# Attention with a top-128 MLP: the exponentials split at column 1024, the TensorE transposes moved up among the scores, weighted sums five blocks behind the scores, query tiles of 512 columns

## The chip, the cores and the metric

The kernel runs on one core of a Trainium2 chip. The metric is the device time of one execution in microseconds; of several executions the median counts. TensorE does matmuls (PE in the profile, its weight loads are PEld), VectorE is DVE, ScalarE is ACT, GpSimd is POOL, and SyncE (SP) issues the DMAs.

## The reference

Four images are attended to, each with N = 12288 queries of C = 128 and 768 keys. The keys, which are the values too, are the 4x4 means of `kv`, projected. Then, for each image, the 128 rows with the highest gate score go through an MLP.

```python
kv_pool = kv.reshape(B, H // r, r, W // r, r, C).mean(axis=(2, 4))
k = v = kv_pool.reshape(B, -1, C) @ w_sr
s = scale * (q @ k.transpose(0, 2, 1))
a = np.exp(s - s.max(-1, keepdims=True))
a /= a.sum(-1, keepdims=True) + 1e-09
x = a @ v                                        # (4, 12288, 128)
scores = np.einsum('bsd,d->bs', x, w_gate)
out = x.copy()
for b in range(B):
    top_idx = np.argpartition(-scores[b], capacity)[:capacity]   # capacity = 128
    xe = x[b, top_idx]
    ye = np.maximum(xe @ w1, 0.0) @ w2
    g = 1.0 / (1.0 + np.exp(-scores[b, top_idx]))
    out[b, top_idx] = xe + g[:, None] * ye
```

## The kernel before

A block is 256 queries (`QT` = 2 groups of 128). An image has 48 blocks, the program 192, which one loop takes in order. Each turn of the loop holds steps of three different blocks.

**The scores of block i+1** (`S`, tile `s`) go into one of two PSUM buffers of three banks, 1536 columns wide: columns 0 to 767 are the first 128 queries against 768 keys, 768 to 1535 the second. Four parts are written one after the other: part 3 (1024:1536), 2 (768:1024), 1 (512:768), 0 (0:512). Each part is three matmuls, since the queries and the keys are split into a high f32r and a low bf16 half (`qh`, `ql`, `kh`, `kl`; `kb` is the key in bf16): `kl,qh`, `kb,ql` and `kh,qh`; parts 2 and 0 do `kh,qh` first.

**The weights of block i.** `s_max` (DVE, tile `m`) takes the maximum of each row over all 1536 columns. Three exponentials on ACT follow: part 1 is 768:1280 into `am`, part 2 is the last 256 columns (1280:1536), part 0 is 0:768 into `am`. `CUT` is 1280. In the first three images (`by_pe`, 144 blocks) part 2 goes into a tile `ae`, and TensorE transposes it in two steps (`turn_pe`, `s<-cst,ae`) back into the PSUM columns 1280:1536. ACT casts these to f16 and DVE takes the bf16 rest (`at<-s`, `at<-s,at`): these weights then stand in the tile `at` already transposed. The other 1280 columns are cast to f16 on ACT (`hl<-am`), POOL subtracts for the bf16 rest (`hl<-am,hl`), and two DMA transposes (`turn`) bring both halves into `at`. In the last image the DMA transposes all 1536 columns, and TensorE transposes none.

**The weighted sums of block i-4** (`AV`, tile `o_two`): 36 matmuls with the transposed weights from `at` as stationary and the values `vx` as moving operand. `LAG` is 4, and `at` has 5 buffers. DVE then normalises (`rz`, `x`), and every second block a DMA stores 512 rows.

**Queries.** `qraw` are tiles of 2048 columns (8 blocks) in two buffers. Every second block one DMA of 512 columns is to load its quarter of a tile, eight blocks ahead.

**Around it.** Steps of four other jobs are put in at named points of the loop (`at_point`): the next image's keys (`next_keys`: loads, 4x4 sums on POOL, projection on TensorE) and values (`v_split`), and for the image before, the search for the top 128 (`topk`: an integer key per row, two searches by bits, each a compare and count on DVE and a matmul, then `pick`) and the MLP. The PSUM room of these jobs is in the score buffer that is not in use (`borrow`).

The order on PE, DVE, ACT and POOL is the order of the program: `InOrder` chains each instruction to the one before it on its engine, and since it is the helper through which all of them go, they all stand at L52 in the profile. DMAs don't go through it: a scheduler sets the order of SP's queue from the buffers' dependencies.

After the loop a tail takes the sums of the last blocks into borrowed PSUM areas (`dest`, `spare`), and then the last image's search and MLP, with nothing beside them.

Of the kernel before, what the change touches and what calls it, by code (L numbers as in the profile page):

```python
# [6 lines left out]
F32 = mybir.dt.float32  # L7
# [9 lines left out]
HALF = 256  # L17
PSUM = bass.MemoryType.PSUM

P = 128  # L20
B, N, C = 4, 12288, 128
HK, WK, R = 384, 32, 4
M = (HK // R) * (WK // R)
KT = M // P
TAPS = R * R
CHUNK = 2048
JPC = CHUNK // P
NCH = N // CHUNK
QT = 2
BLK = QT * P  # L30
NBLK = N // BLK
BPC = CHUNK // BLK
VC = C + 2
# [33 lines left out]
def attention_topk_mlp(ctx, tc, a, outs, capacity):  # L67
    nc = tc.nc
# [4 lines left out]
    kvp = ctx.enter_context(tc.tile_pool(name="kvp", bufs=3))  # L73
    kvs = ctx.enter_context(tc.tile_pool(name="kvs", bufs=2))
    keys = ctx.enter_context(tc.tile_pool(name="keys", bufs=2))
    qp = ctx.enter_context(tc.tile_pool(name="qp", bufs=2))
    qs = ctx.enter_context(tc.tile_pool(name="qs", bufs=3))
    wk = ctx.enter_context(tc.tile_pool(name="wk", bufs=3))
    wke = ctx.enter_context(tc.tile_pool(name="wke", bufs=2))
    hlp = ctx.enter_context(tc.tile_pool(name="hlp", bufs=4))  # L80
    at = ctx.enter_context(tc.tile_pool(name="at", bufs=5))
    ob = ctx.enter_context(tc.tile_pool(name="ob", bufs=3))
    sm = ctx.enter_context(tc.tile_pool(name="sm", bufs=4))
    tk = ctx.enter_context(tc.tile_pool(name="tk", bufs=2))
# [44 lines left out]

    qraw = {}  # L130

    def load_q(b, ch, lo=0, hi=CHUNK):
        if (b, ch) not in qraw:
            qraw[b, ch] = qp.tile([P, CHUNK], F32, name="q_raw")
        nc.sync.dma_start(out=qraw[b, ch][:, lo:hi], in_=a["q"][:, b, ch, lo:hi])

    kvset = {}

# [75 lines left out]

    def first_keys():
        new_keys(0)
        load_q(0, 0, 0, 2 * BLK)
        raws = [load_kv(0, kc) for kc in range(3)]
        nc.sync.dma_start(out=cst, in_=a["cst"])
        raws += [load_kv(0, kc, 2) for kc in range(3, KT)]  # L220
        load_q(0, 0, 2 * BLK, CHUNK)
        split_q(0, 0)
        kv = kvset[0]
        for kc in range(KT):
# [93 lines left out]
    xt_ = {}  # L318

    def split_q(b, blk):  # L320
        ch, h = divmod(blk, BPC)
        raw = qraw[b, ch][:, h * BLK:(h + 2) * BLK]
        qh = qs.tile([P, 2 * BLK], F32R, name="qh")
        ql = qs.tile([P, 2 * BLK], BF16, name="ql")
        act.copy(qh, raw)
        pool.tensor_tensor(out=ql, in0=raw, in1=qh.bitcast(F32), op=ALU.subtract)
        for i in range(2):
            h, l = (x[:, i * BLK:(i + 1) * BLK] for x in (qh, ql))
            qsplit[b, blk + i] = h, h.bitcast(BF16).rearrange("p (q s) -> p q s", s=2)[:, :, 1], l
# [23 lines left out]
    def by_pe(n):  # L353
        return blocks[n][0] < B - 1

    def exp(n, part):
        lo, hi, j = ((0, M, 0), (M, CUT, 1), (CUT, 2 * M, 1))[part]
        if part == 1:
            st[n]["a"] = wk.tile([P, CUT], F32, name="am")
            st[n]["hl"] = hlp.tile([P, 2, QT * M], U16, name="hl")  # L360
            st[n]["at"] = at.tile([P, 2, QT * KT, P], U16, name="at")
        s = s_flat[n % 2][:, lo:hi]
        if part == 2:
            out = s
            if by_pe(n):
                out = st[n]["ae"] = wke.tile([P, HALF], F32, name="ae")
        else:
            out = st[n]["a"][:, lo:hi]
        r = act.activation(out, s, AF.Exp, bias=st[n]["m"][:, j:j + 1])
        if part == 0:  # L370
            st[n]["exp0"] = r.ins
            if "low" in st[n]:
                tc.declare_no_dep(r.ins, st[n]["low"], reason="both only read, other banks")

    def turn_pe(n):
        for c in range(2):
            lo = CUT + c * P
            r = pe.transpose(s_flat[n % 2][:, lo:lo + P], st[n]["ae"][:, c * P:(c + 1) * P], ident)
            tc.declare_no_dep(r.ins, st[n]["exp0"], reason="other banks")

    def halves(n, part):
        lo, hi = ((0, CUT), (CUT, 2 * M))[part]
        a = s_flat[n % 2][:, lo:hi] if part else st[n]["a"]
        if part and by_pe(n):
            hl = [st[n]["at"][:, h, CUT // P:].rearrange("p t q -> p (t q)") for h in range(2)]
        else:
            hl = [st[n]["hl"][:, h, lo:hi] for h in range(2)]
        return a, hl[0].bitcast(F16), hl[1].bitcast(BF16)
# [238 lines left out]

    start(vals, first_values())
    nb = len(blocks)
    LAG = 4  # L630
    for i in range(nb):
        old = i >= LAG
        b, blk = blocks[i]
        if blk % 2 == 0 and i + BPC < nb:
            nb_, nblk = blocks[i + BPC]
            load_q(nb_, nblk // BPC, nblk % BPC * BLK, (nblk % BPC + 2) * BLK)
        if blk == 0 and b + 1 < B:
            start(prep, next_keys(b + 1))
        if i:
# [20 lines left out]
        bank0 = list(InOrder.seen)  # L660
        if more:
            S(i + 1, (3,), bank0 + bank1)
            S(i + 1, (2,), bank0)
        exp(i, 1)
        exp(i, 2)
        if by_pe(i):
            exp(i, 0)
            turn_pe(i)
        if more:
            S(i + 1, (1,), bank0)  # L670
            S(i + 1, (0,))
        to_high(i, 1)
        if old:
# [1 line left out]
            recip(i - LAG)  # L675
            finish(i - LAG)
        to_low(i, 1, dve)
        if not by_pe(i):
            exp(i, 0)
        to_high(i, 0)  # L680
        turn(i, 0)
        to_low(i, 0, pool)
# [8 lines left out]
    n = nb - 1  # L691
    b = blocks[n][0]
    spare = [s_buf[(n + 1) % 2][:, 2 * k:2 * k + 2].rearrange("p k q -> p (k q)")[:, 0:QT * VC].rearrange("p (j c) -> p j c", j=QT) for k in range(3)]
    dest = {n - 3: o_all, n - 2: spare[0], n - 1: spare[1], n: spare[2]}

    def out(m):
        for j in range(QT):
# [20 lines left out]
    for j in range(3):  # L718
        pool.memset(jt[:, j:j + 1], float(j + 1))

    for m in (n - 3, n - 2):
        out(m)
        norm(m)
        put(m)
# [84 lines left out]
```

## Time and profile before

| | us |
|---|---|
| median of three runs (977.23 to 986.22) | 981.31 |
| profiled execution, its own time | 983.61 |
| its span in the trace | 981.8 |
| PE busy | 908.2 |
| PEld busy (beside PE) | 729.7 |
| POOL busy | 749.9 |
| ACT busy | 729.5 |
| DVE busy | 699.7 |

The engines' rows are busy times, so what an engine waits for is not in them. The reduction `m` on DVE runs once a block, and the distance from one `m` to the next is called a block's period here.

### The profile page before, as it was taken

The numbers are of one execution on the slowest core, as the hardware profiler recorded it, in microseconds if no ns is written. First come the engines' busy times: TensorE is split into PE (matmuls) and PEld (weight loads), VectorE is DVE, ScalarE is ACT, GpSimd is POOL, SyncE is SP. The second block draws the span as 40 slices with busy tenths as digits, with TensorE's granted clock in tenths as the row PEclk, the third lists the DMA queues.
The fourth block names the chain that finished last, engine by engine and source line by source line (L and its number), as shares of the span: only waits on it lengthen the run. The fifth ranks groups of instructions, "written<-read, shape, count | busy, mean of one in ns | idle before, by whom it ended". The sixth has DMA issues, their size and how long they took to land.

```text
span 981.8 us, 26115 instructions
## 1 busy us (share of the span) xinstructions
PE 908.2 (93%) x10067; PEld 729.7 (74%) x10067; DVE 699.7 (71%) x1732; ACT 729.5 (74%) x1177; POOL 749.9 (76%) x573
## 2 busy tenths in 40 slices
PE   3889999999989999998999998999999999999944
PEld 2668777787768787776787876877787887777743
DVE  6456666666668777776767776777768887878674
ACT  2567887877967877877877866878789988988700
POOL 1478889888778988987888887898778877777600
PEclk9999999999989999999999999999999999999966
DMA  9999999999999999999989999999999999999910
GB/s 357 227 190 220 241 220 224 244 242 236 225 203 186 249 226 219 233 230 225 235 169 210 236 218 226 207 199 203 199 184 245 224 242 244 231 235 234 225 40 6
DMA packets 600508, 211.31 MB, mean 215 GB/s; under 512 B 532288, under 2 KB 582592, under 8 KB 599616
## 3 DMA queue, kind: packets, MB, share of 16 engines
q1 hardware_dynamic: 600128, 209.12, 104.4%
q8 instruction: 79, 1.29, 0.6%
q0 software_dynamic: 256, 0.52, 0.2%
q14 instruction: 45, 0.37, 0.1%
HBM read 52.04 MB, written 25.43 MB: 79 GB/s over the span
## 4 chain that ended last, share of the span: by engine, by line
PE 56%; DVE 13%; ACT 9%; DMA 8%; issue 4%; POOL 3%; SPq 1%; POOLq 0%; ACTq 0%; DVEq 0%
PE s L52 31%; PE o_two L52 25%; DVE m L52 8%; DMA at<-hl 7%; ACT am L52 5%; POOL hl L52 1%; DVE junk L52 1%; ACT ae L52 1%; ACT hl L52 1%; ACT at L52 1%; POOL ql L52 1%; DVE at L52 1%; DMA xe<-out,idx 1%; POOL kv_sum L52 1%; ACT s L52 1%
## 5 line engine op out<-in xcount | busy, mean ns | idle before, releaser
L52 POOL TENSOR_TENSOR hl<-am,hl 128x1280 bf16<-128x1280 f32 x192 | 503.7, 2623 | 153.6 <-ACT hl L52 75.4
L52 PEld LDWEIGHTS <-at 128*128 128x128 f16 (+1 forms) x6912 | 415.5, 97 | 71.4 <-DMA at<-hl 22.5
L52 PE MATMUL o_two<-vx,at 128*128 128x130 f16 x6804 | 435.0, 220 | 17.5 <-DMA at<-hl 12.9
L52 ACT ACTIVATE am<-s,m 128x512 f32<-128x512 f32 (+1 forms) x384 | 305.4, 795 | 140.6 <-DVE m L52 80.9
L52 DVE TENSOR_REDUCE m<-s 128x2 f32<-128x1536 f32 x192 | 337.1, 1756 | 24.8 <-PE s L52 20.8
L52 PE MATMUL s<-kl,qh 128*128 128x512 bf16 (+1 forms) x768 | 253.3, 333 | 0.0
L52 PE MATMUL s<-kh,qh 128*128 128x512 f32 (+1 forms) x768 | 251.8, 409 | 0.0
L52 PE MATMUL s<-kb,ql 128*128 128x512 bf16 (+1 forms) x768 | 248.7, 327 | 0.5 <-POOL ql L52 0.4
L52 ACT CAST hl<-am 128x1280 f16<-128x1280 f32 x192 | 245.1, 1276 | 1.5
L52 DVE TENSOR_TENSOR at<-s,at 128x256 bf16<-128x256 f32 x144 | 61.1, 425 | 132.5 <-ACT at L52 124.4
L52 PEld LDWEIGHTS s<-kh,qh 128*128 128x128 f32 x768 | 131.6, 192 | 30.5 <-issue 0.6
L52 POOL TENSOR_TENSOR ql<-q_raw,qh 128x512 bf16<-128x512 f32 x96 | 122.5, 1276 | 6.8 <-ACT qh L52 6.8
L52 PEld LDWEIGHTS <-qh 128*128 128x128 bf16 x768 | 75.3, 98 | 63.2 <-issue 62.4
L52 DVE TENSOR_TENSOR x<-o_two,rz 128x260 f32<-128x260 f32 x189 | 81.0, 429 | 10.0
L52 PEld LDWEIGHTS <-ql 128*128 128x128 bf16 x768 | 76.2, 99 | 3.7 <-POOL ql L52 1.1
L52 DVE TENSOR_SCALAR rz<-o_two,sg 128x2 f32<-128x2 f32 x189 | 41.1, 218 | 40.2 <-PE o_two L52 39.3
L52 PE MATMUL s<-cst,ae 128*128 128x128 f32 x288 | 61.6, 296 | 8.4 <-ACT ae L52 7.7
L52 ACT ACTIVATE ae<-s,m 128x256 f32<-128x256 f32 x144 | 67.3, 467 | 0.0
L52 ACT CAST at<-s 128x256 f16<-128x256 f32 x144 | 54.5, 379 | 16.4 <-PE s L52 15.0
L52 ACT CAST qh<-q_raw 128x512 fp32r<-128x512 f32 x96 | 60.6, 631 | 1.1 <-DMA q_raw<-in_q 1.1
L52 PEld LDWEIGHTS s<-cst,ae 128*128 128x128 f32 x288 | 30.4, 141 | 32.0 <-ACT ae L52 31.4
L52 POOL TENSOR_TENSOR kv_sum<-kv_raw 128x256 f32<-128x256 f32 x72 | 52.4, 727 | 0.0
(164 smaller groups left out, 557.4 us busy)
## 6 DMA issues: line engine op xcount, KB each, us to landing
out<-x SPq DMA_DIRECT2D x96, 256.0 KB, 3.4
q_raw<-in_q SPq DMA_DIRECT2D x93, 256.0 KB, 3.8
kv_raw<-in_kv SPq DMA_DIRECT2D x36, 512.0 KB, 5.4
kv_raw<-in_kv SPq DMA_DIRECT2D x6, 1024.0 KB, 7.4
at<-hl SPq DMA_TRANSPOSE x384, 4.0
w<-in_w SPq DMA_DIRECT2D x2, 512.0 KB
q_raw<-in_q SPq DMA_DIRECT2D x1, 768.0 KB, 7.6
cst<-in_cst SPq DMA_DIRECT2D x1, 320.0 KB
```

Of the source, the lines that this page charges most:

```text
L52: r = f(*args, **kwargs)
```

## The change

Three things are changed.

1. In the first three images the exponentials are split into 1024:1536 (512 columns), 768:1024 (256) and 0:768, all into `am`, which is now 1536 columns wide; `ae` and its pool are gone. The two TensorE transposes come right behind score part 3 of the next block and read `am`; score parts 2, 1 and 0 follow them. Exponential 0:768 moves on ACT behind the cast `at<-s`, and behind DVE's subtraction in the program. In the last image the splits stay as they were.
2. `LAG` is 5 instead of 4, `at` has 6 buffers, and the tail does one more block.
3. Each 512 query columns are a tile of their own (four buffers of 512 instead of two of 2048).

```diff
-    qp = ctx.enter_context(tc.tile_pool(name="qp", bufs=2))
+    qp = ctx.enter_context(tc.tile_pool(name="qp", bufs=4))
-    wke = ctx.enter_context(tc.tile_pool(name="wke", bufs=2))
-    at = ctx.enter_context(tc.tile_pool(name="at", bufs=5))
+    at = ctx.enter_context(tc.tile_pool(name="at", bufs=6))
...
-    def load_q(b, ch, lo=0, hi=CHUNK):
-        if (b, ch) not in qraw:
-            qraw[b, ch] = qp.tile([P, CHUNK], F32, name="q_raw")
-        nc.sync.dma_start(out=qraw[b, ch][:, lo:hi], in_=a["q"][:, b, ch, lo:hi])
+    def load_q(b, blk):
+        ch, h = divmod(blk, BPC)
+        qraw[b, blk] = qp.tile([P, 2 * BLK], F32, name="q_raw")
+        nc.sync.dma_start(out=qraw[b, blk], in_=a["q"][:, b, ch, h * BLK:(h + 2) * BLK])
...
     def exp(n, part):
-        lo, hi, j = ((0, M, 0), (M, CUT, 1), (CUT, 2 * M, 1))[part]
+        early = by_pe(n)
+        lo, hi, j = ((0, M, 0), (M, 1024 if early else CUT, 1), (1024 if early else CUT, 2 * M, 1))[part]
...
+        out = s if part == 2 and not early else st[n]["a"][:, lo:hi]
         r = act.activation(out, s, AF.Exp, bias=st[n]["m"][:, j:j + 1])
...
     def turn_pe(n):
+        st[n]["apart"] = []
         for c in range(2):
             lo = CUT + c * P
-            r = pe.transpose(s_flat[n % 2][:, lo:lo + P], st[n]["ae"][:, c * P:(c + 1) * P], ident)
-            tc.declare_no_dep(r.ins, st[n]["exp0"], reason="other banks")
+            r = pe.transpose(s_flat[n % 2][:, lo:lo + P], st[n]["a"][:, lo:lo + P], ident)
+            st[n]["apart"].append(r.ins)
...
-    LAG = 4
+    LAG = 5
...
             S(i + 1, (3,), bank0 + bank1)
-            S(i + 1, (2,), bank0)
-        exp(i, 1)
-        exp(i, 2)
+        exp(i, 2 if by_pe(i) else 1)
         if by_pe(i):
-            exp(i, 0)
             turn_pe(i)
+        exp(i, 1 if by_pe(i) else 2)
         if more:
-            S(i + 1, (1,), bank0)
+            S(i + 1, (2, 1), bank0)
             S(i + 1, (0,))
         to_high(i, 1)
...
         to_low(i, 1, dve)
-        if not by_pe(i):
-            exp(i, 0)
+        exp(i, 0)
         to_high(i, 0)
...
-    dest = {n - 3: o_all, n - 2: spare[0], n - 1: spare[1], n: spare[2]}
+    spare.append(s_buf[n % 2][:, 4:6].rearrange("p k q -> p (k q)")[:, 0:QT * VC].rearrange("p (j c) -> p j c", j=QT))
+    dest = {n - 4: o_all, n - 3: spare[0], n - 2: spare[1], n - 1: spare[2], n: spare[3]}
...
-    for m in (n - 3, n - 2):
+    for m in range(n - LAG + 1, n - 1):
```

What stands on TensorE in one ordinary block, before. `s_110` is the score buffer that the next block's scores go into and `s_111` the one of the block in hand; `cst` holds the identity for a transpose. The waits in brackets name the engine.

```order
L52 MATMUL s_110<-kh,qh 128x512
L52 MATMUL s_110<-kh,qh 128x256
L52 LDWEIGHTS qh
L52 MATMUL s_110<-kl,qh 128x256
L52 LDWEIGHTS ql
L52 MATMUL s_110<-kb,ql 128x256
L52 MATMUL s_111<-cst,ae 128x128 [waits DVE_49,Activation_49]
L52 MATMUL s_111<-cst,ae 128x128
L52 LDWEIGHTS qh
L52 MATMUL s_110<-kl,qh 128x256
```

And the same place after, where the buffers are called `s_107` and `s_108`.

```order
L52 MATMUL s_107<-kh,qh 128x512
L52 MATMUL s_108<-cst,am 128x128 [waits Activation_49]
L52 MATMUL s_108<-cst,am 128x128
L52 MATMUL s_107<-kh,qh 128x256
L52 LDWEIGHTS qh
L52 MATMUL s_107<-kl,qh 128x256
L52 LDWEIGHTS ql
L52 MATMUL s_107<-kb,ql 128x256
L52 LDWEIGHTS qh
L52 MATMUL s_107<-kl,qh 128x256
```

The two transposes stood behind the three matmuls of score part 2; now they stand ahead of them, right behind part 3, and read the tile of the first exponential instead of the second one's.

What stands on ACT in one block, before.

```order
L52 ACTIVATE am<-s_110,m 128x512 [waits DVE_49,Pool_49]
L52 ACTIVATE ae<-s_110,m 128x256
L52 ACTIVATE am<-s_110,m 128x768
L52 CAST at<-s_110 128x256 [waits PE_49]
L52 CAST hl<-am 128x1280 [waits DMAHW5_49,DMAHW4_49,Activation_49]
```

And after.

```order
L52 ACTIVATE am<-s_107,m 128x512 [waits DVE_49,Pool_49]
L52 ACTIVATE am<-s_107,m 128x256
L52 CAST at<-s_107 128x256 [waits PE_49]
L52 ACTIVATE am<-s_107,m 128x768
L52 CAST hl<-am 128x1280 [waits DMAHW7_49,DMAHW6_49,Activation_49]
```

The cast `at<-s` stood behind the 768-column exponential; now it stands ahead of it, and the large exponential comes just ahead of the large cast.

What stands in SP's queue where the queries are loaded, before.

```order
L402 DMA_TRANSPOSE at<-hl 128x10x128 x2
L135 DMA q_raw<-in_q 128x512 x4
L402 DMA_TRANSPOSE at<-hl 128x10x128 x2
L438 DMA out<-x 128x4x128
L402 DMA_TRANSPOSE at<-hl 128x10x128 x4
L438 DMA out<-x 128x4x128
```

And after.

```order
L134 DMA q_raw<-in_q 128x512
L434 DMA out<-x 128x4x128
L398 DMA_TRANSPOSE at<-hl 128x10x128 x4
L134 DMA q_raw<-in_q 128x512
L434 DMA out<-x 128x4x128
L398 DMA_TRANSPOSE at<-hl 128x10x128 x4
```

The four query loads of a 2048-column tile stood in one bunch between two blocks' transposes, since its buffer comes free at once; now one load stands in every two blocks.

## Rows read from the trace of the kernel before

**Rows 1.** The page's own parts 1 and 2: the span, the busy time of each engine, and the busy share of the DMA engines in 40 equal slices of the span (9 is 90% or more).

```profile
span 981.8 us, 26115 instructions
PE 908.2 (93%) x10067; PEld 729.7 (74%) x10067; DVE 699.7 (71%) x1732; ACT 729.5 (74%) x1177; POOL 749.9 (76%) x573
DMA  9999999999999999999989999999999999999910
```

**Rows 2.** The table by windows, all instructions. The columns: the window in us, its length, then the busy time (and count) of PE, PEld, DVE, ACT and POOL, the granted TensorE clock as a share of full speed, the DMA share and GB/s. The second window begins at the `m` of block 5 and ends at that of block 144, the third ends at that of block 191; the last is the tail.

```profile
60.35:715.73 655.38, 639.33 (x7151) 510.75 (x7149) 471.92 (x1062) 512.60 (x837) 558.48 (x432) 0.99 1.10 220
715.73:921.54 205.81, 200.18 (x2332) 162.53 (x2330) 162.35 (x384) 182.43 (x274) 158.81 (x101) 1.00 1.16 228
```

**Rows 3.** The timeline of one ordinary block, cut to DVE's `m`, ACT, and the matmuls and weight loads around the TensorE transposes. The columns: start in us, how long, engine, line, operation, out<-in, shapes, count; in brackets the idle time just before and what ended it.

```profile
91.92 1.76 DVE L52 TENSOR_REDUCE m<-s 128x2 f32<-128x1536 f32 x1
...
93.78 0.69 ACT L52 ACTIVATE am<-s,m 128x512 f32<-128x512 f32 x1 [0.68 <-DVE m L52]
...
94.36 0.47 ACT L52 ACTIVATE ae<-s,m 128x256 f32<-128x256 f32 x1
...
94.57 0.28 PE L52 MATMUL s<-kl,qh 128*128 128x256 bf16 x1
...
94.69 0.27 PE L52 MATMUL s<-kb,ql 128*128 128x256 bf16 x1
94.72 0.90 ACT L52 ACTIVATE am<-s,m 128x768 f32<-128x768 f32 x1
94.88 0.20 PEld L52 LDWEIGHTS s<-cst,ae 128*128 128x128 f32 x2 [0.20 <-ACT ae L52]
...
95.16 0.27 PE L52 MATMUL s<-kl,qh 128*128 128x256 bf16 x1
...
95.50 0.38 ACT L52 CAST at<-s 128x256 f16<-128x256 f32 x1
...
95.75 1.29 ACT L52 CAST hl<-am 128x1280 f16<-128x1280 f32 x1
95.92 0.42 DVE L52 TENSOR_TENSOR at<-s,at 128x256 bf16<-128x256 f32 x1 [0.99 <-ACT at L52]
...
96.37 1.76 DVE L52 TENSOR_REDUCE m<-s 128x2 f32<-128x1536 f32 x1
```

**Rows 4.** Groups of weight loads of the whole span, by shape: count, then busy us and mean ns of one, then idle time before them and what ended it.

```profile
L52 PEld LDWEIGHTS s<-kh,qh 128*128 128x128 f32 x768 | 131.6, 192 | 30.5 <-issue 0.6
L52 PEld LDWEIGHTS s<-cst,ae 128*128 128x128 f32 x288 | 30.4, 141 | 32.0 <-ACT ae L52 31.4
```

**Rows 5.** The table of waits of the whole span: the waiting engine, tile and line, then what it waited for, the sum in us, how often, the longest.

```profile
PEld s L52 <- ACT ae L52: 31.4, 112, 3.8
...
PEld L52 <- DMA at<-hl: 22.5, 29, 2.7
...
PE o_two L52 <- DMA at<-hl: 12.9, 22, 2.2
```

**Rows 6.** The timeline around block 120: a bunch of query loads on SP, and two waits of TensorE's weight loads in that block.

```profile
593.17 2.22 SPq L135 DMA_DIRECT2D q_raw<-in_q  x4
...
602.53 0.68 PEld L52 LDWEIGHTS <-at 128*128 128x128 f16 x12 [1.74 <-DMA at<-hl]
...
604.40 0.35 PEld L52 LDWEIGHTS <-at 128*128 128x128 bf16 x6 [1.19 <-DMA at<-hl]
```

**Rows 7.** The timeline of block 4, whose weighted sums are the first of the program: its `m`, and the two waits of TensorE for the values `vx`.

```profile
50.72 1.76 DVE L52 TENSOR_REDUCE m<-s 128x2 f32<-128x1536 f32 x1
...
52.27 0.22 PE L52 MATMUL o_two<-vx,at 128*128 128x130 f16 x1 [0.76 <-ACT vx L52]
...
54.72 2.52 PE L52 MATMUL o_two<-vx,at 128*128 128x130 f16 x27 [2.23 <-POOL vx L52]
```

**Rows 8.** The timeline of DVE in two of the 28 blocks (numbers 16 to 142) in which another DVE instruction delays the next `m`: the first of them from its `m` to the next, with that instruction, and the last of them, its `m` and the next.

```profile
110.11 1.76 DVE L52 TENSOR_REDUCE m<-s 128x2 f32<-128x1536 f32 x1 [0.20 <-PE s L52]
...
114.44 0.41 DVE L52 TENSOR_REDUCE mx<-kv_proj 128x1 f32<-128x256 f32 x1
...
114.77 1.75 DVE L52 TENSOR_REDUCE m<-s 128x2 f32<-128x1536 f32 x1
...
706.54 1.75 DVE L52 TENSOR_REDUCE m<-s 128x2 f32<-128x1536 f32 x1
...
711.21 1.75 DVE L52 TENSOR_REDUCE m<-s 128x2 f32<-128x1536 f32 x1
```

**Rows 9.** The timeline at the beginning of the first search for the top 128 (block 52), DVE and POOL, and the same DVE instruction in the tail, with 92 columns in place of 96.

```profile
279.82 2.62 POOL L52 TENSOR_TENSOR hl<-am,hl 128x1280 bf16<-128x1280 f32 x1
279.96 2.59 DVE L52 TENSOR_TENSOR key<-key,sc 128x96 int32<-128x96 int32 x1
...
930.84 0.26 DVE L52 TENSOR_TENSOR key<-key,sc 128x92 int32<-128x92 int32 x1
```

**Rows 10.** The timeline of PE in the tail: the weighted sums of the last four blocks, but for the second of them, which didn't wait.

```profile
925.10 2.22 PE L52 MATMUL o_two<-vx,at 128*128 128x130 f16 x36 [0.97 <-DVE x L52]
...
930.36 2.22 PE L52 MATMUL s<-vx,at 128*128 128x130 f16 x36 [0.97 <-DVE x L52]
933.36 0.85 PE L52 MATMUL s<-vx,at 128*128 128x130 f16 x12 [0.77 <-DMA at<-hl]
934.71 1.55 PE L52 MATMUL s<-vx,at 128*128 128x130 f16 x24 [0.49 <-DMA at<-hl]
```

## What the change is forecast to do, before its time was known

> **What bounds the kernel now.** I read the page's totals first. TensorE is busy 93% of the span, POOL 76%, ACT 74%, DVE 71%, and the DMA engines are at 90% or more in nearly every slice [rows 1]. A busy share of 93% leaves little, so the question is where a block takes more than its ordinary time. The windows give that: 139 blocks in 655.38 us are 4.71 a block, and 47 blocks of the last image in 205.81 are 4.38 [rows 2].
>
> The timeline of an ordinary block shows what 4.45 consists of, and that it is a closed chain over three engines [rows 3]. From `m` (91.92) to the first exponential (93.78) it is 1.86. The second starts 0.58 later and takes 0.47, so it ends at 94.83. The TensorE transposes' weight load starts 0.05 behind that. From there to the first matmul of score part 1 (95.16) it is 0.28, and from that to the next `m` (96.37) 1.21. The sum is 1.86 + 0.58 + 0.47 + 0.05 + 0.28 + 1.21 = 4.45. The table of waits agrees: the transposes wait for the exponential `ae` in 112 of 144 blocks [rows 5]. DVE is nearly on this chain too: its subtraction `at<-s,at` ends at 96.34, 0.03 ahead of the next `m`.
>
> So 139 blocks hold 655.4 - 139 x 4.45 = 37 us above the ordinary, in places: late DMA transposes, DVE work that comes ahead of `m`, key projections, the search's first step. The change can win there, and in the ordinary block only if the chain gets shorter.
>
> **Part 1, split and moved transposes, the ordinary block.** The transposes now wait for the first exponential (0.69) and no longer for two. Their load is ready at 1.86 + 0.69 + 0.05 = 2.60 behind `m` instead of 2.96, a gain of 0.36. But score part 2, which filled the wait, now stands behind them: three matmuls, 0.12 apart by the starts at 94.57 and 94.69, are 0.36. The new chain is 2.60 + 0.28 + 0.36 + 1.21 = 4.45: **no change in 112 blocks**. Bounds: the weight load waited 0.20 in this block, of which the 0.05 stays, so TensorE can win at most 0.15 a block; and it can lose 0.19, if the load of `kh,qh`, 192 ns [rows 4], stands free behind the transposes. I take 0, since the two steps cancel by rows of the same block.
>
> **DVE's side.** The cast `at<-s` moves ahead of the 768-column exponential. It started 0.62 behind the transposes' load, about 0.13 of that behind the exponential. With 0.36 + 0.13, DVE's subtraction ends 0.49 earlier (an estimate from [rows 3]). In the ordinary block TensorE still releases `m`, and nothing comes of it. It counts in the 28 blocks where another DVE instruction (`mx`, `sg`, `rest`, `mask`, `ge` and the like) stands between this subtraction and `m`: the first has a period of 4.66, the last of 4.67 [rows 8], 0.21 and 0.22 too long. Over the 28, with each excess cut at 0.49, the sum is 8.4. I take **-6**, since some of these blocks have TensorE projections too; bounds 0 and -8.4.
>
> The large cast `hl<-am` pays for it. It started 3.83 behind `m`. Now the cast `at<-s` starts at 2.60 + 0.49 = 3.09, the exponential 0.25 behind it, the large cast 0.78 behind that (both distances as in [rows 3]), so at 4.12: 0.29 later. POOL's 2.62 and the DMA transposes wait for it. Part 2 hides this: they get 4.45 more. Without that cover it would come on top of every late transpose.
>
> **Part 2, one block more of lag; part 3, queries one by one.** TensorE's weight loads wait 22.5 us for DMA transposes in 29 cases, 2.7 at most [rows 5]. The timeline shows why: four query loads go out in a bunch at 593.17, the transposes queue behind them, and TensorE waits 1.74 and 1.19 within one block some 9 us later [rows 6]. Now one query load stands between two blocks' transposes, and a transpose may come a whole period (4.45) later than before, more than the longest wait. Of the 22.5, 0.77 + 0.49 lie in the tail [rows 10]. A block that waits here doesn't wait for the exponential again, so 0.15 is given back in each of 29: 22.5 - 1.3 - 4.4 = 17. I take **-17**. Bounds: -12.9, if only the matmuls' own waits count [rows 5], and -22.5.
>
> The start: block 4, the first with weighted sums, waits 0.76 and 2.23 for `vx` and takes 60.35 - 50.72 = 9.63 [rows 2, 7]; behind the wait 27 matmuls take 2.52 [rows 7], where the tail has 36 in 2.22 [rows 10]. With one block more of lag its place is filled by the warming matmuls, and `vx` was there at 54.72, before the next block's `m` at 50.72 + 4.45 = 55.17. That is 9.63 - 4.45 = **-5.2**; at least the two waits, -3.0.
>
> The tail does one more block of sums with nothing beside it: 2.22, and 0.97 for one more wait for `x` [rows 10]. The waits for transposes there (0.77, 0.49) vanish. 2.22 + 0.97 - 1.26 = **+1.9** (1.0 without the second wait, 3.2 with the old ones).
>
> **The search's key.** In block 52 a DVE instruction of 0.26 takes 2.59: it starts at 279.96, and ends with the POOL instruction that started at 279.82 [rows 9]. That is 2.33 more, in one of three images. The lag moves the step one block further on, and nothing fixes what POOL does then. I take **-2**, one such delay less; bounds of two delays either way, -5 and +5. The Trainium skill, "SBUF — State Buffer", section "SBUF: two separate sides", says that DVE and GpSimd share a port pair as an exclusive lock held for a whole instruction, when DVE reads two SBUF operands and GpSimd reads SBUF too. The trace agrees in this row (2.59 beside 2.62). By that rule alone the step is caught whenever POOL is at work, 85% of the time (558.48 of 655.38 [rows 2]); the term would be 0 then and the sum 2 higher.
>
> **The sum.** -6 - 17 - 5.2 + 1.9 - 2 = -28.3 on 983.61, the profiled execution's own time, which is 2.3 above the median of the runs: 955.3 there, **953** against the median.
>
> **Rivals.** (a) *The weight load behind the transposes stands free.* `kh,qh` needs 192 ns against 141 for a transpose's load [rows 4], and now it can hide only behind short transposes, where before it ran beside 512-column matmuls. At 0.19 in 112 blocks it is +21: 974. Against it: weight loads run beside matmuls everywhere else. The Trainium skill, "TensorE: Matmul & The Clock Gate", section "LDWEIGHTS", gives P / 1.2 ns, by estimate 107 for 128 columns whatever their type; then this rival would cost +12. The rows with f32 weights (192) say more.
>
> (b) *The DMA engines lack rate, not order.* They are full in every slice and their share is 1.10 to 1.16 [rows 1, 2]. If lateness builds up as fast as before, five blocks hide one period once: -4.5 in place of -17, so 966. Against it: the longest waits follow a bunch [rows 6].
>
> (c) *TensorE gains its wait after all:* -0.15 in 112 blocks, -17, so 936.
>
> (d) *Slower: POOL becomes the bound.* The large cast starts 0.29 later in each block, while POOL has 4.45 - 558.48 / 139 = 0.43 idle a block. If `hl`'s four buffers or the order on POOL bring this delay back into the chain, each of 143 blocks grows by 0.29, which is 41: 953 + 41 = 994, and 1017 if the gains by cover (17 and 6) go too. It decides from the point at which POOL's idle time ahead of `hl<-am,hl` falls to zero. Against it: 0.29 is less than 0.43, and nothing in a block waits for POOL but the transposes.
>
> (e) *The lag doesn't help where I think,* since the waits named DMA come from late casts, and little changes: within 1%.
>
> **How the numbers follow.** Forecast 0.55, (a) 0.12, (b) 0.13, (c) 0.10, (d) 0.05, (e) 0.05. The forecast's own bounds are -22.5 - 8.4 - 5.2 - 5 + 1.0 = -40, 941, and -12.9 - 0 - 3.0 + 5 + 3.2 = -8, 973; the ends are unlikely together. The range of 940 to 973 takes in (b) and most of (a), and leaves out (c) and (d). A measurement of this kernel tells about 1% (10 us) from no change. Faster by more than that is below 971.5: the forecast but for its upper end (0.52), (b), (c) and a third of (a), 0.79; slower is (d) with part of (e), 0.07; the rest, 0.14, is within 1%.
>
> **What would show it.** In the profile after: the distance from `m` to `m` in ordinary blocks 4.45, and the transposes' wait, now for `am`, still there but short. No wait of weight loads for `at<-hl` above 0.5 before the tail. Query loads on SP one by one. Block 4 at 4.5 to 5. The subtraction `at<-s,at` ending about 0.5 ahead of `m`. POOL idle ahead of `hl<-am,hl` still, waiting for ACT. What would make it wrong: an ordinary block that isn't 4.45, since 0.1 there is 14 us, more than any other term but the DMA's; and waits for `at<-hl` that come back.

## The result: 989 us instead of the 953 forecast, a little slower than before

The changed kernel takes 989.08 us against 982.21 before (medians of 20 runs each), a ratio of 1.007 with an interval of 1.005 to 1.009. It lies outside the range given and on the other side. The few runs that lie more than 1.5% above the fastest of their kernel (one of the changed kernel's here, three of e6's below) are left out of every ratio and interval, and of the median given for e6. The profiled execution has a span of 987.7 us, 5.9 more than before. The page's totals say little, as before: ACT and DVE are somewhat busier, POOL is as busy as it was, TensorE a little less [rows 1].

```profile
span 987.7 us, 25937 instructions
PE 897.8 (91%) x9922; PEld 726.5 (74%) x10103; DVE 710.9 (72%) x1732; ACT 755.2 (76%) x1177; POOL 749.1 (76%) x573
```

The windows answer to [rows 2], and the columns are the same. The first row holds the first five blocks, the second the tail; the two rows behind the dots go from block 5's `m` to block 144's, and on to block 191's.

```profile
29.60:54.26 24.66, 21.34 (x233) 16.80 (x238) 13.27 (x26) 20.04 (x35) 16.39 (x15) 1.00 0.77 174
925.90:987.70 61.80, 32.89 (x345) 29.18 (x342) 36.11 (x238) 7.29 (x13) 10.65 (x14) 0.72 0.38 69
...
54.26:715.31 661.05, 631.92 (x7010) 508.22 (x7147) 486.31 (x1062) 537.97 (x836) 558.83 (x433) 1.00 1.10 219
715.31:925.90 210.59, 199.50 (x2298) 163.55 (x2333) 159.47 (x385) 182.30 (x275) 157.83 (x100) 1.00 1.17 225
```

The same two stretches of the kernel before, the first five blocks and the tail:

```profile
29.22:60.35 31.13, 25.09 (x238) 19.82 (x238) 14.08 (x29) 19.80 (x35) 17.71 (x16) 0.89 0.91 186
921.54:981.80 60.26, 31.66 (x309) 27.90 (x306) 35.59 (x235) 7.09 (x13) 9.58 (x12) 0.71 0.29 62
```

The first five blocks gained 6.5 (24.66 against 31.13) and the tail lost 1.5, both near the forecast. The 139 blocks lost 5.7 (661.05 against 655.38) and the last image 4.8 (210.59 against 205.81), where 25 were to be won; the first `m` comes 0.4 later, which makes up the 5.9. The table of waits shows in what [rows 5]:

```profile
PEld s L52 <- ACT am L52: 55.6, 120, 1.9
...
ACT hl L52 <- DMA at<-hl: 38.5, 29, 2.8
...
PEld L52 <- DMA at<-hl: 22.4, 29, 2.1
...
PE o_two L52 <- DMA at<-hl: 12.3, 20, 1.6
```

TensorE waits for DMA transposes as long as before (22.4 and 12.3), in spite of a whole block more of lag. And a wait that before's table didn't have is the largest of those for transposes: ACT's cast `hl<-am` waits 38.5 us until an older block's transposes have left one of the four `hl` buffers. So the transposes are not as late as before but a block later still. (The wait in the first line, of the TensorE transposes for `am`, is the one in the chain of every ordinary block.) The period of block 37 shows both waits at once (ACT, PE, PEld):

```profile
201.70 1.26 ACT L52 CAST hl<-am 128x1280 f16<-128x1280 f32 x1 [2.54 <-DMA at<-hl]
...
201.64 1.55 PE L52 MATMUL o_two<-vx,at 128*128 128x130 f16 x24 [1.64 <-DMA at<-hl]
...
201.64 1.38 PEld L52 LDWEIGHTS <-at 128*128 128x128 bf16 x24 [1.81 <-DMA at<-hl]
```

SP's timeline shows where the time goes. The quickest transposes hold SP for 1.25 us, the median one for 1.54. Behind a query load and a store, the four transposes of two blocks hold it here for 7.24:

```profile
181.56 0.54 SPq L134 DMA_DIRECT2D q_raw<-in_q  x1
182.19 0.40 SPq L434 DMA_DIRECT2D out<-x  x1
182.69 7.24 SPq L398 DMA_TRANSPOSE at<-hl  x4
190.02 0.53 SPq L134 DMA_DIRECT2D q_raw<-in_q  x1
```

Over the span the 384 transposes hold SP for 713 us, 676 before (summed from the trace). Two blocks of 4.45 have 8.9 us; load, store and four transposes take 8.5 of them here, and each key load on top (the next one is at 191.09) puts the queue further back. In block 35 the cast ended 5.54 behind `m`, and its transpose was issued 17.90 behind `m`.

### The profile page after: what moved, and what is told of

It reads as the page before. It is cut to its first block, busy times and chain, and to the rows that moved or that the text cites. A ratio compares the mean times of both kernels' runs of the same rounds, so it can differ in the third digit from the quotient of the medians.

```text
span 987.7 us, 25937 instructions
## 1 busy us (share of the span) xinstructions
PE 897.8 (91%) x9922; PEld 726.5 (74%) x10103; DVE 710.9 (72%) x1732; ACT 755.2 (76%) x1177; POOL 749.1 (76%) x573
## 4 chain that ended last, share of the span: by engine, by line
PE 49%; DMA 15%; ACT 12%; DVE 11%; issue 7%; POOL 5%; SPq 1%; POOLq 0%; ACTq 0%; DVEq 0%
PE s L52 27%; PE o_two L52 22%; DMA at<-hl 13%; ACT am L52 5%; DVE m L52 4%; POOL hl L52 4%; ACT hl L52 3%; DVE junk L52 1%; DMA kv_raw<-in_kv 1%; ACT at L52 1%; DVE pooled L52 1%; POOL ql L52 1%; POOL kv_sum L52 1%; DVE at L52 1%; SPq L398 1%
## 5 line engine op out<-in xcount | busy, mean ns | idle before, releaser
L52 POOL TENSOR_TENSOR hl<-am,hl 128x1280 bf16<-128x1280 f32 x192 | 503.9, 2624 | 166.4 <-ACT hl L52 112.3
L52 PEld LDWEIGHTS <-at 128*128 128x128 f16 (+1 forms) x6912 | 412.4, 97 | 71.3 <-DMA at<-hl 22.4
L52 PE MATMUL o_two<-vx,at 128*128 128x130 f16 x6768 | 430.1, 219 | 15.3 <-DMA at<-hl 12.3
L52 ACT ACTIVATE am<-s,m 128x512 f32<-128x512 f32 (+1 forms) x528 | 358.3, 706 | 71.9 <-DVE m L52 40.7
L52 PE MATMUL s<-kh,qh 128*128 128x512 f32 (+1 forms) x768 | 285.4, 423 | 0.3 <-ACT hs L52 0.2
L52 ACT CAST hl<-am 128x1280 f16<-128x1280 f32 x192 | 241.6, 1259 | 30.6 <-DMA at<-hl 24.4
L52 PE MATMUL s<-kb,ql 128*128 128x256 bf16 (+1 forms) x697 | 213.2, 321 | 6.1
L52 PE MATMUL s<-kl,qh 128*128 128x256 bf16 (+1 forms) x658 | 203.0, 324 | 0.0
L52 PE MATMUL s<-cst,am 128*128 128x128 f32 x288 | 61.4, 295 | 13.8 <-ACT am L52 13.5
L52 PEld LDWEIGHTS s<-cst,am 128*128 128x128 f32 x288 | 30.9, 140 | 56.5 <-ACT am L52 53.7
L52 DVE TENSOR_TENSOR hl<-s,hl 128x256 bf16<-128x256 f32 x48 | 20.4, 425 | 38.6 <-ACT hl L52 35.1
```

What stands on the lines that cost most here:

```text
L52: r = f(*args, **kwargs)
```

## The experiments

Ratios are against the kernel before, run beside each; the interval is in brackets. In the diffs, `...` marks what is as shown above or plays no part in the argument.

**One part alone.** e1 is part 2, e2 part 3, e3 part 1; e4 is the change without part 3.

```diff
 e1:
-    LAG = 4
+    LAG = 5
 ...
+    hsp = ctx.enter_context(tc.tile_pool(name="hsp", bufs=1))
-            hs = tk.tile([P, FT, P], F32, name="hs")
+            hs = hsp.tile([P, FT, P], F32, name="hs")
```

> The kernel before with part 2 alone: five blocks of lag, six at buffers and the longer tail (the MLP's tile hs gets a pool of its own with one buffer, to make room). Two theories of why the change gained nothing. Theory S: SP's queue and the DMA engines behind it are the limit; each group of loads ahead of the transposes stretches them, and query loads one by one, beside the stores, stretch more of them than bunches of four. Then the lag alone gains its start (5 us) and one period of backlog, less the tail's 2: 982 - 5 - 4 + 2 = 975, and waits for at<-hl stay. Theory C: the large cast, later by 0.45 us in each block, is what makes the transposes late; the lag itself does what the prediction said. Then 982 - 5 - 17 + 2 = 962.

Measured 975.74, 0.9941 [0.9921, 0.9962]. The time is theory S's (975). TensorE's weight loads wait 5.2 us for transposes, not 22.5, but the cast waits 17.3.

e2 has `load_q` and the pool `qp` of the change in the kernel before.

```diff
 e2:
-    qp = ctx.enter_context(tc.tile_pool(name="qp", bufs=2))
+    qp = ctx.enter_context(tc.tile_pool(name="qp", bufs=4))
 ...
+        qraw[b, blk] = qp.tile([P, 2 * BLK], F32, name="q_raw")
```

> The kernel before with part 3 alone: query tiles of 512 columns, one load every two blocks. Theory S: slower than before by 5 to 15 (987 to 997), with more time in the transposes' issue on SP (676 us before, 713 after) and more waits for at<-hl. Theory C: the query loads no longer come in a bunch, so the waits for at<-hl shrink: 965 to 978.

Measured 974.56, 0.9932 [0.9907, 0.9957]: **query loads one by one are a gain**, as the prediction had it, and theory S falls in this form. The transposes hold SP for 664 us, less than before.

e3 has `exp`, `turn_pe` and the loop's order of the change in the kernel before.

```diff
 e3:
-        exp(i, 1)
-        exp(i, 2)
+        exp(i, 2 if by_pe(i) else 1)
 ...
-        if not by_pe(i):
-            exp(i, 0)
+        exp(i, 0)
```

> The kernel before with part 1 alone: other splits of the exponentials, transposes moved, lag 4, query tiles of 2048. Theory S: the cast's 0.45 us is little beside a backlog of 10 us; DVE's gain of up to 8 stays: 976 to 984. Theory C: every transpose is 0.45 us later, 144 times, where it is late already: 990 to 1000.

Measured 980.03, 0.9991 [0.9964, 1.0018]: no difference, so theory C falls too.

```diff
 e4 (against the changed kernel):
-    qp = ctx.enter_context(tc.tile_pool(name="qp", bufs=4))
+    qp = ctx.enter_context(tc.tile_pool(name="qp", bufs=2))
 ...
```

> The changed kernel without part 3: query tiles of 2048 columns in two buffers, as before (hs in a pool of its own with one buffer, to make room). Theory S: what the split query loads cost comes back: 965 to 978. Theory C: the cast is late as in the changed kernel: 985 to 995, no gain from the loads.

Measured 972.64, 0.9918 [0.9878, 0.9958]. No part does harm alone, and parts 1 and 2 together gain; all three lose. Something clashes.

**Which two clash.** SP's order tells. With lag 4 a store becomes ready in odd blocks and the query load is issued in even ones; with lag 5 both fall into even ones and stand side by side.

```diff
 e5 (against the changed kernel):
-    LAG = 5
+    LAG = 4
 ...
 e6 (against the kernel before): part 2 and part 3
 ...
+    LAG = 5
 ...
 e7 (against the changed kernel):
-    hlp = ctx.enter_context(tc.tile_pool(name="hlp", bufs=4))
+    hlp = ctx.enter_context(tc.tile_pool(name="hlp", bufs=5))
 ...
```

> The changed kernel without part 2: lag 4, five at buffers, the old tail. The parts alone gained 6 (lag), 7 (query tiles) and 2 (split) of 982, and lag with split 9; all three together lose 7. Theory A (adjacent): lag and query tiles clash. With lag 5 a store becomes ready in the same block as the query load, so SP issues 512 KB in one go in every two blocks and the four transposes behind them are stretched; with lag 4 the store and the load stand two transposes apart. Then this kernel, without the clash, takes 970 to 977. Theory H (buffers): the transposes are late all the same, and hl's four buffers with the later cast turn it into waits on ACT. Then the query tiles with the split lose here too: 984 to 992.

> The changed kernel without part 1: lag 5 and query tiles of 512, exponentials and transposes as before. Theory A: the clash is here too, 983 to 992. Theory H: the cast is early again, 965 to 975.

> The changed kernel with five hl buffers instead of four (hs in a pool of its own with one buffer, to make room). Theory A: the queue's backlog only grows one period further before somebody waits, and at's six buffers and the lag bind as before: 984 to 990. Theory H: ACT's wait of 38 us for the transposes goes: 960 to 975.

e5 measured 977.13, 0.9933 [0.9906, 0.996]; e6 988.9, 1.0058 [1.001, 1.0106]; e7 991.6, 1.0108 [1.004, 1.0176]. All three go theory A's way and none theory H's, though e5 lies 0.1 and e7 1.6 above A's range: lag with query tiles is the pair, with or without the split, and one more buffer only moves the wait: ACT's is gone, TensorE's weight loads wait 36.0 in place of 22.4. One thing in e5 is not theory A's: its weight loads still wait 23.1 us for transposes, against 9.3 in e2, which differs by part 1 alone. With lag 4 nothing covers the later cast, as the prediction said of one without cover. The times of the two are the same (0.9933 and 0.9932).

**The neighbours themselves.** e8 changes nothing but SP's order: the load is issued behind an even block's transposes and gets an order-only dependency on the second of them. e9 does the same to e5, where it makes neighbours of what was apart.

```diff
 e8 (against the changed kernel; e9 the same against e5):
+        r = nc.sync.dma_start(out=qraw[b, blk], in_=a["q"][:, b, ch, h * BLK:(h + 2) * BLK])
+        if behind is not None:
+            tc.add_manual_dep(r.ins, behind, mybir.DependencyInfo(mybir.DependencyClass.NoSync, mybir.DependencyReason.DATA), reason="SP order")
 ...
-        if blk % 2 == 0 and i + BPC < nb:
-            load_q(*blocks[i + BPC])
 ...
+        last = turn(i, 1).ins.name
+        if blk % 2 == 0 and i + 8 < nb:
+            load_q(*blocks[i + 8], last)
```

> The changed kernel with one order changed: each query load is put behind the transposes of an even block in SP's queue, so that store, two transposes, load, two transposes alternate instead of load, store, four transposes. Nothing else moves. Theory A: the clash goes, and with it 15 to 25 us: 964 to 974, the best of all; the transposes' issue time on SP falls from 713 to under 670 us. Theory H: no change, 985 to 993.

> The changed kernel with lag 4 (as e5), and with each query load put behind the transposes of an even block in SP's queue; with lag 4 this makes load and store neighbours (load, store, four transposes), where e5 has them apart. The mirror of e8. Theory A (neighbours are what costs): 10 to 20 slower than e5's 977, so 987 to 997, though the lag is the old one. If the lag itself did the harm, or the moved load did the good in e8: 972 to 980.

e8 measured 972.28, 0.9896 [0.9838, 0.9954]; e9 998.41, 1.0175 [1.0118, 1.0232], 1.4 above theory A's range. The same move gains 17 where it parts load and store and loses 21 where it joins them (by the medians against the changed kernel and e5; by the ratios 1.7% and 2.4%). The transposes hold SP for 658 us in e8 and 713 in e9. SP's timeline of e8 and of e9:

```profile
314.72 0.54 SPq L436 DMA_DIRECT2D out<-x  x1
315.36 4.10 SPq L400 DMA_TRANSPOSE at<-hl  x2
319.51 0.57 SPq L134 DMA_DIRECT2D q_raw<-in_q  x1
320.19 3.08 SPq L400 DMA_TRANSPOSE at<-hl  x2
```

```profile
184.04 0.58 SPq L134 DMA_DIRECT2D q_raw<-in_q  x1
184.71 0.40 SPq L436 DMA_DIRECT2D out<-x  x1
185.22 7.48 SPq L400 DMA_TRANSPOSE at<-hl  x4
```

These rows show the order. They don't show the cost: the two pairs of e8 add up to 7.18, next to nothing less than the 7.24 above. The cost is in the means, taken from the traces between blocks 5 and 144. Four transposes behind load and store hold SP for 6.84 in the changed kernel (47 cases) and 6.83 in e9 (55). Two behind the store alone and two behind the load alone hold it for 3.10 and 3.17 in e8, 3.13 and 3.21 in e5 (62 cases each), so 6.3 for four. The difference lies in the first transpose, 2.18 behind both in the changed kernel and 1.6 behind one of them in e8.

In e8 the waits shrink to what the prediction wanted: all of the weight loads' 6.5 lies in the tail. The windows between the same `m` (blocks 5, 144 and 191) are 14.4 and 7.6 shorter than in the changed kernel:

```profile
PEld L52 <- DMA at<-hl: 6.5, 5, 2.2
...
ACT hl L52 <- DMA at<-hl: 3.7, 5, 1.6
```

```profile
54.68:701.31 646.63, 633.66 (x7149) 508.44 (x7147) 484.36 (x1062) 539.51 (x836) 559.03 (x433) 1.00 1.12 223
701.31:904.27 202.96, 199.73 (x2335) 163.39 (x2333) 161.56 (x385) 182.50 (x275) 158.09 (x100) 1.00 1.19 232
```

One more view speaks on rival (b), that the DMA engines lack rate. In the same stretch of 53.5 us, in which the changed kernel's queue was behind all the time, its engines were less busy and moved less than e8's. The changed kernel, then e8 (the last two columns are DMA share and GB/s):

```profile
181.50:235.00 53.50, 49.83 (x549) 40.00 (x558) 34.14 (x60) 40.73 (x62) 43.80 (x33) 1.00 1.10 218
```

```profile
181.50:235.00 53.50, 53.34 (x602) 42.95 (x599) 36.23 (x64) 45.21 (x70) 46.72 (x35) 1.00 1.19 228
```

**Part 1 and the place of the search.** In blocks 121 to 150, in which neither TensorE's weight loads nor ACT's cast waits for a transpose in any of these kernels, the sum of the periods is 138.8 before, 140.1 in e3, 140.0 in e1, and 141.5 in the changed kernel and e8. e10 to e14 ask why; all have the query loads between the transposes, as e8.

```diff
 e10 (against e8):
-        if old and blocks[i - LAG][1] == NBLK - 1:
-            start(select, topk(blocks[i - LAG][0]))
+        if i > LAG and blocks[i - LAG - 1][1] == NBLK - 1:
+            start(select, topk(blocks[i - LAG - 1][0]))
 e11: e10 without part 1      e12: e8 without part 1      e14: e13 and e10
 e13 (against e8):
         exp(i, 1 if by_pe(i) else 2)
+        if by_pe(i):
+            exp(i, 0)
 ...
         to_low(i, 1, dve)
-        exp(i, 0)
+        if not by_pe(i):
+            exp(i, 0)
```

> e8 (loads between the transposes) with one more edit: the search for the top 128 starts one block later. With lag 5 its steps had moved from blocks of one parity to those of the other, where ACT and POOL also split queries; blocks 121 to 150, without a wait for DMA, sum to 141.5 in the changed kernel and e8, to 139.4 in e5 with lag 4. Theory P (parity): that sum goes back to 139.5, and over three images 4 to 6 us are gained: 966 to 969. If the place of the steps has nothing to do with it: 972 as e8.

> e10 without part 1: lag 5, query tiles of 512 with the loads between the transposes, the search one block later, but exponentials and transposes as before. In blocks 121 to 150 the split alone costs 1.3 us, and it helps in none of the long stretches. If the split is worth nothing: 964 to 970, at or below e10, and blocks 121 to 150 sum to 138.8. If the split pays (DVE's earlier subtraction, 6 us forecast): 972 to 976.

> e8 without part 1: lag 5, query tiles of 512 with the loads between the transposes, search where the changed kernel starts it, exponentials and transposes as before. It prices part 1 with the queue in order. Theory D (the split pays on DVE's side, as forecast, 6 us): 976 to 980, against e8's 972. Theory L (the split delays ACT's large cast by 0.45 us, and what stands behind the cast in ACT's queue reaches the next block's first exponential late): the blocks with extra ACT work get shorter again (block 48 4.52 in place of 4.95; blocks 121 to 150 sum to 140.0 in place of 141.5), 966 to 971.

> e8 with one ACT instruction moved in the first three images: the 768-column exponential goes ahead of the cast at<-s, so that it fills ACT's wait for the TensorE transposes; the splits and the early transposes stay. Theory L: the large cast starts at 3.85 behind m again, block 48 goes from 4.95 to 4.5, blocks 121 to 150 from 141.5 to about 140, in all 4 to 6 us: 966 to 969. Theory D: DVE's subtraction is late again and the 28 blocks lose up to 8: 976 to 980.

> e13 and e10 together: 768-column exponential ahead of the cast, and the search for the top 128 one block later. If both effects add: 963 to 967. If the later search brings back what it cost with the old split (the key step behind POOL in blocks 54 and 102, 3.5 us each, and the clash in blocks 92 and 140): 970 to 980.

| | us | ratio | blocks 121 to 150 |
|---|---|---|---|
| e10 | 969.98 | 0.9886 [0.983, 0.9942] | 140.5 |
| e11 | 983.14 | 1.0016 [0.9992, 1.004] | 142.0 |
| e12 | 966.58 | 0.9861 [0.9838, 0.9884] | 140.0 |
| e13 | 972.6 | 0.9921 [0.9898, 0.9944] | 139.9 |
| e14 | 980.07 | 0.9998 [0.9971, 1.0026] | 141.8 |

e10 lies between its two theories: its sum is 1.0 shorter than e8's where 2 were expected, its runs overlap e8's, and so what the place of the search is worth stays open. e12 is the fastest of all, below both kernels: lag and query tiles with the loads in order, and **without part 1**. Its sum over blocks 121 to 150 is 1.5 shorter than e8's, as theory L has it; the whole times of e8 and e12 have overlapping intervals. e13 shows the mechanism within one block. This is ACT in block 48 of the changed kernel, then of e13:

```profile
255.39 1.26 ACT L52 CAST hl<-am 128x1280 f16<-128x1280 f32 x1
256.55 0.50 ACT L52 ACTIVATE kv_proj<-kv_proj,sg 128x256 f32<-128x256 f32 x1
257.09 0.41 ACT L52 CAST vx<-kv_proj 128x256 f16<-128x256 f32 x1
257.40 0.61 ACT L52 CAST qh<-q_raw 128x512 fp32r<-128x512 f32 x1
257.92 1.04 ACT L52 ACTIVATE am<-s,m 128x512 f32<-128x512 f32 x2
```

```profile
249.57 1.29 ACT L52 CAST hl<-am 128x1280 f16<-128x1280 f32 x1
...
252.13 1.84 ACT L52 ACTIVATE am<-s,m 128x512 f32<-128x512 f32 x3
```

The `m` of this block is at 255.56 in the changed kernel, and at 250.19 in e13. The first exponential starts 2.36 and 1.94 behind it: the large cast is late by 0.45, three other ACT instructions stand behind it in the queue, and the exponential behind those. The period is 4.95 in the changed kernel, 4.53 in e13, 4.52 before.

e13 as a whole is no faster than e8, e11 and e14 lose what they should have won. In each of them single blocks of 7.9 to 9.2 appear (118 in e13; 54, 92, 102 and 140 in e11 and e14), and each is a case like that of [rows 9]: a DVE instruction beside POOL's large subtraction. Block 118 in e13 (DVE and POOL), then the same two instructions in e12:

```profile
581.20 2.72 DVE L52 SCALAR_TENSOR_TENSOR rest<-key,junk 128x96 f32<-128x96 uint16 x1
...
581.18 2.62 POOL L52 TENSOR_TENSOR hl<-am,hl 128x1280 bf16<-128x1280 f32 x1
```

```profile
581.01 0.26 DVE L52 SCALAR_TENSOR_TENSOR rest<-key,junk 128x96 f32<-128x96 uint16 x1
...
581.05 2.70 POOL L52 TENSOR_TENSOR hl<-am,hl 128x1280 bf16<-128x1280 f32 x1
```

In e13 it starts 0.02 us behind POOL's instruction and takes 2.46 longer than in e12, where it starts 0.04 ahead of it. Block 92 of e11 (DVE and POOL) has another instruction of the search, 0.34 long by the median:

```profile
461.98 2.69 DVE L52 SCALAR_TENSOR_TENSOR oh<-cst,ecx,ge 96x128 bf16<-96x128 f32 x1
...
461.88 2.65 POOL L52 TENSOR_TENSOR hl<-am,hl 128x1280 bf16<-128x1280 f32 x1
```

Block 140 reads the same, and in blocks 54 and 102 it is the key step (2.72 and 4.62); e14 has the same four. In all eight the DVE instruction ends 0.12 to 0.15 behind POOL's subtraction. These four blocks alone sum to 33.0 in e11 and in e14, against 19.1 in e12.

## Why the prediction was wrong, step by step

**The ordinary block: right, but for the large cast.** Its period is 4.45, and the transposes' weight load starts 2.59 behind `m` (2.60 forecast). DVE's subtraction ends 0.56 ahead of `m` (0.5 forecast). Rival (a) and rival (c) are out. One such block (DVE's `m`, PEld, ACT, DVE):

```profile
85.77 1.76 DVE L52 TENSOR_REDUCE m<-s 128x2 f32<-128x1536 f32 x1 [0.55 <-PE s L52]
...
88.36 0.20 PEld L52 LDWEIGHTS s<-cst,am 128*128 128x128 f32 x2 [0.32 <-ACT am L52]
...
89.11 0.91 ACT L52 ACTIVATE am<-s,m 128x768 f32<-128x768 f32 x1
89.24 0.42 DVE L52 TENSOR_TENSOR at<-s,at 128x256 bf16<-128x256 f32 x1 [0.53 <-ACT at L52]
...
90.05 1.26 ACT L52 CAST hl<-am 128x1280 f16<-128x1280 f32 x1
90.22 1.76 DVE L52 TENSOR_REDUCE m<-s 128x2 f32<-128x1536 f32 x1 [0.56 <-PE s L52]
```

The large cast starts 4.28 behind `m`, 0.45 later than before, not 0.29. The prediction put 0.78 between the 768-column exponential and the cast, the distance that it had read between this exponential and the cast `at<-s`, which doesn't read its result. The large cast does read it, and comes 0.94 behind it.

**Start and tail: right in size.** -6.5 and +1.5, where -5.2 and +1.9 stood in the sum. Block 4 takes 4.96 in place of 9.63, which is -4.7. Another -2.0 comes from block 1 (7.07 before, 5.09 after), which no term forecast.

**The DMA term: wrong in sign.** -17 was the largest term, and its failing step is the sentence "Now one query load stands between two blocks' transposes". The order printed ahead of the prediction shows load, store and four transposes. The load was looked at alone, and not with its new neighbour; that lag 5 moves the store by one block, into the block of the load, was nowhere in the working. In place of -17 the waits of weight loads stayed (22.4 against 22.5), and ACT's cast waited 38.5 more. Parted from the store (e8), the loads and the lag bring the waits of weight loads from 22.5 to 6.5, and the whole kernel is 17 below the changed one. So the mechanism existed, but the change came with a cost of the same size.

The size was too large as well. e12 is the kernel before with lag, query tiles and parted loads, and in it the weight loads' waits ahead of the tail fall from 20.9 to 0.3. Between blocks 5 and 144 it takes 643.09 and so wins 12.3, of which 5.3 are the key's (blocks 52 to 54); in the last image it takes 204.30 and wins 1.5. That leaves about 8.5 for the DMA term, half of -17. It is an estimate, since the search's steps have moved in e12 too.

The step "a transpose may come a whole period (4.45) later than before" left something out too: the `hl` buffers. Four of them were enough for lag 4; with lag 5 the cast of block i waits for block i-4's transposes ahead of TensorE. e7 shows that more buffers cure nothing while the queue falls behind.

Rival (b) had the pattern, lateness that builds up until the further block is used up, but not the time (966) nor, as far as is known, the reason: engines that move 218 GB/s where those of e8 move 228 are not held up by their rate, and a new order alone cures it. Rival (e), late casts and a time within 1%, has the time by luck: e8 leaves the casts where they are, and the waits go. In the last image, where all 1536 columns go by DMA, waits for transposes remain in e8 and e12 as well (ACT's cast, 3.7 and 5.5); whether rate or order limits there is open.

**DVE's side: wrong.** -6 was forecast, and the failing step is that the 0.49 by which DVE's subtraction ends earlier was counted in each of the 28 blocks as if nothing else moved. Block 16, the example of [rows 8], is 4.66 before and 4.72 after (103.94 to 108.66 below). Before, the first exponential started 1.85 behind `m`, as in an ordinary block:

```profile
111.96 0.69 ACT L52 ACTIVATE am<-s,m 128x512 f32<-128x512 f32 x1 [0.22 <-DVE m L52]
```

After (ACT, and DVE):

```profile
106.06 1.04 ACT L52 ACTIVATE am<-s,m 128x512 f32<-128x512 f32 x2
...
103.94 1.76 DVE L52 TENSOR_REDUCE m<-s 128x2 f32<-128x1536 f32 x1 [0.55 <-PE s L52]
...
108.02 0.41 DVE L52 TENSOR_REDUCE mx<-kv_proj 128x1 f32<-128x256 f32 x1
108.66 1.76 DVE L52 TENSOR_REDUCE m<-s 128x2 f32<-128x1536 f32 x1 [0.23 <-PE s L52]
```

DVE's gain is there: `mx` ends 0.23 ahead of `m`. But three other ACT instructions stand behind the late cast in this block, so the first exponential starts 2.12 behind `m`, 0.27 later than before, and now TensorE releases the next `m`. The change took one lateness away and made another of the same size. "Part 2 hides this" was true for the late cast's transposes alone: what stands behind the cast on ACT, and who waits for that, was not asked. It costs 0.43 in block 48. In other blocks DVE's earlier instruction runs into POOL: in block 70 of e3 `rest` starts 0.14 behind a POOL instruction of 1.28 and takes 1.25 in place of 0.26.

Over the 27 blocks between 16 and 142, without block 52, in which such an instruction stood last ahead of `m` before, the periods sum to 130.2 before and 131.5 with part 1 alone (e3), to 131.8 in e8 and 129.0 in e12, which is e8 without part 1. So part 1 cost 1.3 and 2.8 there in place of winning 6; it gained nothing alone (e3) and is not in the fastest kernel (e12).

**The key: right in sign, too small.** In block 53 the step takes 1.25, beside a POOL instruction of 1.27, in place of 2.59. Blocks 52 to 54 sum to 14.2 instead of 19.4, so -5.2 where -2 stood. That the step met a shorter POOL instruction is luck of the alignment, as the bounds had it, and e11 and e14 show the other side of it. What the prediction didn't price is TensorE's clock. In the kernel before, the hit left TensorE idle for 3.48, and behind that the granted clock was 0.50, the lower of its two levels (1.2 of 2.4 GHz), for 4.62: blocks 53 and 54 took 5.61 and 5.75. In the changed kernel it stayed at 1.00 there. The row of PE and the window before, then the step after (POOL, DVE):

```profile
285.42 0.69 PE L52 MATMUL s<-cst,ae 128*128 128x128 f32 x2 [3.48 <-ACT ae L52]
```

```profile
285.38:290.00 4.62, 4.58 (x29) 3.59 (x30) 2.18 (x2) 2.87 (x5) 2.37 (x2) 0.50 1.31 195
```

```profile
282.78 1.27 POOL L52 TENSOR_TENSOR kv_sum<-kv_sum 128x512 f32<-128x512 f32 x1
...
282.92 1.25 DVE L52 TENSOR_TENSOR key<-key,sc 128x96 int32<-128x96 int32 x1
```

**The chances.** 0.7% slower falls into "within 1%", which had 0.14; slower by more had 0.07, and the rival on that side was POOL. POOL idles ahead of `hl<-am,hl` as forecast (112.3 us for ACT's cast, 75.4 before); what took the gain away came through the order in SP's queue, which no rival named.

## What to carry to other kernels

When a change moves two things by a block, read the queue they share with both moves made: a load and a store that stood apart may become neighbours, and what stands behind them in the queue pays. A buffer chain has as much slack as its scarcest pool, so a longer lag needs a look at every pool between producer and consumer. Of an instruction that comes later, ask what is queued behind it on its own engine, not only who reads its result: what one engine wins by a new order, another can lose in the same block. And a delay that leaves TensorE idle can cost more than its own length, when the granted clock falls behind it.

## What the runs showed of the hardware that was not expected

Two transfers of 256 KB side by side in SP's queue hold back the transposes behind them a little more than the same two apart: 6.84 and 6.83 us on average for four behind both (the changed kernel and e9), 3.10 and 3.17 for two behind one of them (e8). Over the span that is 713 us against 658, and the kernel that has them apart is 17 faster. What in the chip holds SP there was not shown. A DVE instruction of 0.26 us that starts just behind a POOL instruction ends with it or shortly after, in three cases: 2.59, 1.25 and 2.72 us beside 2.62, 1.27 and 2.62. For the first, the Trainium skill's exclusive lock ("SBUF — State Buffer", section "SBUF: two separate sides") was cited ahead of the result; the other two agree with it. Such a hit can cost more than its length: in the kernel before, TensorE stood idle 3.48 behind it, the granted clock was at 0.50 from 285.38 to 290.00, and blocks 52 to 54 took 19.4 in place of three times 4.45. In e11 the window of block 55, behind the hit of block 54, has a granted clock of 0.72, and the block takes 5.62.
